# A fused Fourier-mixing and product-key-expert kernel: another order for the seven-product groups, routing in seven steps, and other slots for the preparation work

## The chip, the cores and the metric

The kernel runs on one core of one Trainium2 chip, as one launch. The metric is device time in microseconds (us), the median of several runs. TensorE is called PE here, VectorE DVE, ScalarE ACT, GpSimd POOL, and SyncE, which only issues transfers, SP.

## The reference

The input is x with 2048 rows and 512 columns. It is normalised to xn (mean and variance of each row), and three terms are added:

```python
return x + _A_ref(xn, A_dft_seq_re, A_dft_seq_im, A_dft_hid_re, A_dft_hid_im) + _B_ref(xn, B_w_q, B_k1, B_k2, B_u, B_v)
```

`_A_ref` is the real part of a two-dimensional discrete Fourier transform, given by its matrices. `_B_ref` is a layer of 4096 small experts. For each row and each of 32 heads it finds two experts and adds their outputs:

```python
q = jnp.einsum("nd,dhc->nhc", xf, w_q)            # H=32 heads, 2*128 columns
s1 = jnp.einsum("nhd,ed->nhe", q[..., :dk], k1)   # 64 scores
s2 = jnp.einsum("nhd,ed->nhe", q[..., dk:], k2)   # 64 scores
# the best 2 of s1 and of s2 give 4 candidates; the best 2 of their sums
# are the experts top_e = i1*64 + i2, with weights g = softmax(top_s)
act = _gelu(jnp.einsum("nd,nhkd->nhk", xf, u[top_e]))
out = jnp.einsum("nhk,nhk,nhkd->nd", g, act, v[top_e])
```

## The kernel before

The kernel is written with a tile framework: the program issues operations in order, and a scheduler places each engine's instructions by that order as their inputs come ready in its own estimate. On the chip each engine then works through its queue in order, so an instruction that waits holds all that stand behind it on its engine.

The time has four stages.

*Start* (up to some 80 us): normalisation, the Fourier transform by its symmetries, and the first scores.

*Scores* (some 80 to 427 us). The heads are handled in eight chunks of four heads (`NCH`), the rows in 16 tiles of 128 (`NT`). For each chunk j and tile i, `s_mm` (L252) issues 12 matmuls of 128x512 into a PSUM bank (`pa`, four buffers). In `scores` ACT copies the bank to a tile `ss` (L953, four buffers), and DVE takes from it the eight best values of each group of 64 (L957) and their indices (L961). Around that the loop over i issues other work at fixed tiles:

- `m_prep` (L162 and L164 on ACT, L167 on POOL) splits the projection weights of a later chunk into a high and a low half; `m_stage` and `m_mul` (L148, PE) need all four of them (t = 0 to 3) at tiles 3, 4, 5 and 7 of the chunk.
- `routing` turns the values and indices of the chunk that was just finished into two expert numbers and two weights. It came in three parts, issued behind tile 1 (part 0), tile 2 (part 2) and tile 4 (part 1) of the following chunk. In it POOL adds candidates (L886 to L888), DVE compares them (L889, L890), POOL subtracts (L891), ACT takes an Exp (L894), and DVE and POOL form the rest.
- `fill_uv` scales and splits u and v into halves (L780 and L781 on ACT, L782 on POOL) at the numbers in the list `slots`; for u four more POOL operations form sums (L810 to L813), and `split4` five tiles later splits these and stores them to DRAM (`s_d`). `stage_v` does the same for the v groups that stay in DRAM (`v_d`). `todo[n]` lists what is issued behind tile i of chunk j, with n = 16 j + i.

*Pairs* (some 427 to 1100 us). For 16 batches of 128 rows the kernel computes all products of the batch with u (4096 x 128), the phase "z", and the product of a sparse weighting with v, the phase "v". The phases run z0, z1, v0, then for b = 2, 4, ... 14: z(b, b+1), v(b-1), v(b), and at the end v15. A z phase of a pair takes two batches at once. Both factors are split in 2 x 2 blocks, and seven block products take the place of eight (Strassen's scheme in Winograd's form). The groups of u form four quads (`QUADS`), so there are 28 products of 24 matmuls each, issued by `slot` (L1172). A digit names the product and a letter the quad in the order `SEQ`. Products accumulate in three sums of a quad, each in a PSUM bank: X (products 1, 6, 7, 4), Y (2) and Z (5, 3). There are four such banks for all quads and for the sum of a v phase; `take` takes the one that was freed first. What drains them is listed in `work`: ACT copies behind 1 (L1206), 5 (L1211), 6 (L1213) and 7 (L1219), DVE adds behind 2 (L1208), 3 (L1216) and 7 (L1220, which adds what ACT's copy left), and ACT's gelu (L1196) behind 4. Products 3, 6 and 7 use sums of u from `s_d`, loaded into a ring of three tiles by `ring_load`, whose order `ring_plan` works out ahead. Products 1 and 5 and others use sums of x (`x4`, from `t_d`) or x itself (`xb2`), loaded at the start of the phase v(b-2).

A v phase has eight steps of 12 matmuls (L1334, `v_part`). Between the products and these steps the dictionary `plan` puts `g_mm` (DVE builds one-hot factors L, R in L1264, L1269, L1272; PE multiplies them, L1274), `w_part` (DVE L1282 and L1290, ACT L1289) and checks on the transform matrices and weights (`compare`, `fit`), which load tiles `cx` and `fit`. In a phase v(b-2) with even b-2, `w_part` for the batch b-1 is planned behind steps 5 and 7 and `g_mm` behind steps 1, 3 and 7. The last product of a pair, 4d, is issued behind step 0 of v(b-1).

*End* (from some 1100 us): the last v phase and the output.

These lines of the loop over tiles set the order of routing:

```python
if i in (1, 2, 4) and pend is not None:
    routing((0, 2, None, 1)[i - 1], *pend)
if j + 1 == NCH and i in (4, 7, 8):
    routing((4, 7, 8).index(i), j, vals, idx, 0, 4, nc.vector)
```

Of the kernel before, what the change touches and what calls it, by code (L numbers as in the profile page):

```python
# [18 lines left out]
P = 128  # L19
# [5 lines left out]
NCH = 8  # L25
# [11 lines left out]
def tile_fnet_peer(ctx, tc, x, ca, cb, c5, wt, wf, wr, wq, kt, ut, vn, out):  # L37
# [683 lines left out]
    def part_b(safe, stS, stP, stQ, stE, xt, u_sb, cmp_p, w4):  # L721
# [149 lines left out]
        def routing(part, j, vals, idx, t0=0, t1=NT, ge=nc.gpsimd):  # L871
# [11 lines left out]
            if part == 0:  # L883
# [4 lines left out]
                ge.tensor_tensor(c10, a[..., 1], b[..., 0], op=ALU.add)  # L888
                nc.vector.tensor_tensor(pm, c01, c10, op=ALU.is_ge)  # L889
                nc.vector.tensor_tensor(c01, c01, c10, op=ALU.max)  # L890
                ge.tensor_tensor(c00, c01, c00, op=ALU.subtract)  # L891
            elif part == 1:
                ex, g = c10, sp.tile([P, n, 2, HC], F32, tag="g", name=f"g{j}_{t0}", bufs=1)
# [3 lines left out]
                ge.tensor_tensor(g[:, :, 1, :], ex, g[:, :, 0, :], op=ALU.mult)  # L897
                nc.vector.tensor_copy(zi[:, :, 2, :, 0, hs], g)
                nc.vector.tensor_tensor(zi[:, :, 2, :, 1, hs], g, zi[:, :, 2, :, 0, hs], op=ALU.subtract)
            else:  # L900
                iw = sp.tile([P, n, 2, 2 * HC], F32, tag="if", name=f"if{j}_{t0}", bufs=1)
                i1 = iw.rearrange("p i w (k h) -> p i k w h", k=2)
                nc.vector.tensor_copy(iw, idx[:, :, :, 0:2].rearrange("p i w k h -> p i w (k h)"))
                if not safe:
                    v = iw.rearrange("p i w (k h) -> p (i w k) h", k=2)
                    ge.tensor_tensor(v, v, hoff.unsqueeze(1).to_broadcast([P, 4 * n, HC]), op=ALU.subtract)
                    c = j + (t0 > 0)
                    nc.vector.tensor_reduce(bnd[:, 0, c:c + 1], iw, axis=AX.XYZ, op=ALU.min)
                    nc.vector.tensor_reduce(bnd[:, 1, c:c + 1], iw, axis=AX.XYZ, op=ALU.max)
                di = sp.tile([P, n, 2 * HC], F32, tag="di", name=f"di{j}_{t0}", bufs=1)  # L910
# [6 lines left out]
                e = di.rearrange("p i (k h) -> p i k h", k=2).bitcast(I32)  # L917
# [85 lines left out]
        for g, n in zip(range(V2, 16), (25, 38, 41, 57, 73, 89, 102)):  # L1003
# [6 lines left out]
        for j in range(NCH):  # L1010
# [11 lines left out]
            for i in range(NT):  # L1022
# [15 lines left out]
                if i in (1, 2, 4) and pend is not None:  # L1038
                    routing((0, 2, None, 1)[i - 1], *pend)
                if j + 1 == NCH and i in (4, 7, 8):  # L1040
                    routing((4, 7, 8).index(i), j, vals, idx, 0, 4, nc.vector)
# [8 lines left out]
        for part in range(3):  # L1050
# [128 lines left out]
        def z_pair(b, n, after):  # L1179
# [3 lines left out]
            total, done, cg = 1344 * (len(SEQ) - 1), 0, 0  # L1183
            def work(at, o):
                if 1:
# [32 lines left out]
                    elif op == "7":  # L1218
                        nc.scalar.activation(dst(1, 1), v(X), AF.Copy)  # L1219
                        nc.vector.tensor_tensor(dst(1, 1), dst(1, 1), dst(1, 0), op=ALU.add)  # L1220
# [5 lines left out]

            for at, o in enumerate(SEQ[:-1]):
                while late and late[0][0] <= at:
                    late.pop(0)[1]()
                work(at, o)  # L1230
                done += 1344
                while cg < 16 and done * 16 >= (cg + 1) * total:
                    after(cg)
                    cg += 1

            def last():
                while late:
                    late.pop(0)[1]()
                work(len(SEQ) - 1, SEQ[-1])
                while late:  # L1240
                    late.pop(0)[1]()

            plan.setdefault((("v", b[0] - 1), 0), []).insert(0, last)
# [320 lines left out]
        if not safe:  # L1564
            for n in range(len(QUADS)):
                put(("v", 0), n, lambda qd=len(QUADS) - 1 - n: first_sum(qd))
# [32 lines left out]
        if not safe:  # L1599
# [18 lines left out]
            for f, n in ((U, 68), (F[0], NK + 16 - V2), (F[1], 16 + V2)):  # L1618
                assert sum(v.count(f) for v in plan.values()) >= n
        for n, ph in enumerate(phases):  # L1620
            if ph[0] == "z":
                b = ph[1:]
                for c in b:
                    ACT[c] = BT[c] if c < 2 else act_tile(c)
# [4 lines left out]
                if not safe and b[0] in PAIRS and len(b) == 2:  # L1629
                    z_pair(b, PAIRS.index(b[0]), after)  # L1630
# [178 lines left out]
```

## Time and profile before

| | before |
|---|---|
| median of 3 runs | 1151.65 us (1150.69 to 1154.37) |
| profiled execution, its own time | 1148.38 us |
| its span, first to last instruction | 1146.6 us |
| mean granted clock of PE | 0.993 |
| PE busy | 1111.1 us, 97% |
| DVE busy | 970.1 us, 85% |
| ACT busy | 681.0 us, 59% |
| POOL busy | 332.9 us, 29% |
| DMA, mean rate | 192 GB/s |

The table is read from the page of one profiled execution. PE's busy time is the sum over stages in which the same engine does different things, so what a change in one stage can bring is read from the idle time of PE in that stage. In a row of the timeline the first number is the start in us from the start of the span, the second the length in us, and what stands in square brackets is how long the engine stood idle just before and whose work ended that. The granted clock is the share of full speed at which PE was let run. The longer entries in the view of waits give total us, the number of times and the longest.

### The profile page before, as it was taken

What the parts mean: (1) busy time and instruction counts of PE and PEld (TensorE: products, weight loads), DVE (VectorE), ACT (ScalarE), POOL (GpSimd) and SP (SyncE); (2) the same over time, 40 slices, a digit from 0 to 9 for tenths busy, and PEclk for the clock granted to TensorE, in tenths of its full rate; (3) what the DMA queues carried; (4) which work ended last, traced back from release to release, by engine and by line L of the source; (5) the groups of instructions that cost most, each with busy time, mean ns of one, the idle gap of its engine ahead of it and who ended that gap; (6) DMA issues with size and microseconds to landing.
All of it is one profiled execution on the core that took longest, in us unless ns stands there. A gap on an engine that the chain in (4) does not pass through costs nothing.

```text
span 1146.6 us, 29162 instructions
## 1 busy us (share of the span) xinstructions
PE 1111.1 (97%) x11528; PEld 724.2 (63%) x11528; DVE 970.1 (85%) x2904; ACT 681.0 (59%) x1126; POOL 332.9 (29%) x385
## 2 busy tenths in 40 slices
PE   9999899999999999999999999999999999999997
PEld 6455454544445459779478579569559659659643
DVE  7899789899898799884997897898798788788783
ACT  6558498887888565455546546545545546555451
POOL 0429899988899740000000000000000000000000
PEclk8999999999999999999999999999999999999999
DMA  9883546454372325874866766757667667566354
GB/s 297 265 217 147 193 143 208 141 168 148 93 230 84 115 78 180 192 252 147 250 201 220 243 210 229 229 191 252 197 212 252 193 219 252 193 220 206 128 177 121
DMA packets 132273, 220.51 MB, mean 192 GB/s; under 512 B 35092, under 2 KB 71067, under 8 KB 132126
## 3 DMA queue, kind: packets, MB, share of 16 engines
q1 hardware_dynamic: 129520, 214.28, 58.0%
q0 software_dynamic: 2304, 4.20, 2.3%
q8 instruction: 92, 1.51, 0.5%
q14 instruction: 55, 0.45, 0.1%
q10 hardware_dynamic: 302, 0.08, 0.0%
HBM read 183.06 MB, written 29.69 MB: 186 GB/s over the span
## 4 chain that ended last, share of the span: by engine, by line
PE 42%; DVE 17%; DMA 8%; ACT 3%; issue 2%; POOL 2%; SPq 1%; DVEq 0%; ACTq 0%; POOLq 0%
PE z L1172 16%; PE v L1334 10%; PE s L252 9%; DMA cx<-in_cb_dram 4%; PE z L1095 4%; DVE L L1264 4%; DVE w L1282 3%; PE g L1274 2%; DVE act L1290 2%; DMA cx<-in_ca_dram 2%; DVE cx L1382 2%; DMA v<-v_d 1%; DVE w L1290 1%; DVE R L1269 1%; DVE R L1272 1%
## 5 line engine op out<-in xcount | busy, mean ns | idle before, releaser
L252 PE MATMUL s<-m,xq 128*128 128x512 f16 x1344 | 300.1, 382 | 5.4 <-ACT uvpFalse L122 3.1
L1334 PE MATMUL v<-v,act 128*128 128x512 f16 x1044 | 231.8, 379 | 1.4 <-DMA v<-v_d 1.4
L252 PEld LDWEIGHTS <-xq 128*128 128x128 f16 x1344 | 130.5, 99 | 158.3 <-issue 9.9
L1345 POOL DMA_DIRECT2D y<-in_x_dram x16 | 14.4, 898 | 660.9 <-DVE R L1269 144.2
L1334 PEld LDWEIGHTS <-act 128*128 128x128 f16 x1044 | 99.8, 98 | 116.7 <-issue 2.0
L1264 DVE TENSOR_TENSOR L<-io_lam,cmp 128x2048 f16<-128x2048 f16 x128 | 156.3, 1221 | 9.6 <-PE g L1274 9.6
L1172 PEld LDWEIGHTS <-u 128*128 128x128 f16 x2688 | 153.0, 98 | 4.9 <-issue 3.0
L957 DVE MAX8 vals<-ss 128x8 f32<-128x64 f32 x896 | 133.4, 216 | 3.6 <-ACT ss L953 3.5
L1172 PEld LDWEIGHTS <-s 128*128 128x128 f16 x1944 | 110.4, 98 | 8.4 <-issue 8.4
L1334 PE MATMUL v<-v,w 128*128 128x512 f16 x480 | 106.8, 379 | 1.4 <-DMA v<-v_d 1.4
L1408 ACT ACTIVATE cx<-cx 128x896 f32<-128x896 f32 x64 | 60.3, 942 | 62.7 <-DVE cx L1388 45.9
L953 ACT ACTIVATE ss<-s,wsc 128x512 f32<-128x512 f32 x120 | 79.8, 679 | 27.5 <-PE s L252 18.5
L961 DVE FIND_INDEX8 idx<-vals,ss 128x8 uint16<-128x256 f32 x224 | 93.8, 419 | 0.0
L1289 ACT ACTIVATE act<-w 128x1024 f16<-128x1024 f32 x36 | 48.4, 1359 | 63.4 <-DVE w L1282 59.6
L1172 PE MATMUL z<-xb,u 128*128 128x128 f16 x1344 | 84.2, 219 | 0.0
L1172 PE MATMUL z<-x,u 128*128 128x128 f16 x1344 | 81.4, 219 | 2.5 <-ACT act L1219 2.5
L1172 PE MATMUL z<-x,s 128*128 128x128 f16 x1296 | 81.1, 219 | 0.4 <-ACT act L1206 0.4
L1334 PEld LDWEIGHTS <-w 128*128 128x128 f16 x480 | 45.9, 98 | 54.6 <-issue 1.9
L1274 PEld LDWEIGHTS <-L 128*128 128x128 f16 x2048 | 60.7, 96 | 15.7 <-issue 3.7
L1282 DVE SCALAR_TENSOR_TENSOR w<-act,scl,g 128x1024 f32<-128x1024 f32 x44 | 55.9, 1280 | 16.0 <-ACT act L1196 16.0
L1274 PE MATMUL g<-R,L 128*128 128x32 f16 x2048 | 63.4, 176 | 3.9 <-DVE R L1272 3.0
L1196 ACT ACTIVATE act<-act,scl 128x512 f32<-128x512 f32 x56 | 39.8, 719 | 39.8 <-DVE act L1216 17.4
(365 smaller groups left out, 1910.2 us busy)
## 6 DMA issues: line engine op xcount, KB each, us to landing
v<-v_d SPq DMA_DIRECT2D x67, 512.0 KB, 5.1
s<-s_d SPq DMA_DIRECT2D x63, 512.0 KB, 4.4
cx<-in_cb_dram SPq DMA_DIRECT2D x64, 448.0 KB, 6.7
w<-in_wq_dram SPq DMA_DIRECT2D x28, 512.0 KB, 5.1
fit<-in_wq_dram SPq DMA_DIRECT2D x28, 512.0 KB, 3.8
uv<-in_vn_dram SPq DMA_DIRECT2D x16, 512.0 KB, 3.7
uv<-in_ut_dram SPq DMA_DIRECT2D x16, 512.0 KB, 4.1
s_d<-v SPq DMA_DIRECT2D x32, 256.0 KB, 4.2
```

The costliest lines, as they stand in the source:

```text
L252: nc.tensor.matmul(ps, xt[i][:, l, kd, :], m[:, r, kd, :], start=(n == 0), stop=(n == 3 * KD - 1))
L953: nc.scalar.activation(s, ps, AF.Copy, scale=inv)
L957: nc.vector.max(vals[:, i, w, :, h], s[:, g, :])
L961: nc.vector.max_index(idx[:, i, w].rearrange("p k h -> p (k h)"), vals[:, i, w, 0:2].rearrange("p k h -> p (k h)"), s[:, w * HC:g + 1, :]. ...
L1095: nc.tensor.matmul(ps if n == 1 else ps.rearrange("p (b n) -> p b n", b=2), ug[:, l, c % 2, kd, :], xb2[:, k0, r, kd, :] if n == 1 else xb ...
L1172: nc.tensor.matmul(bank[:, t * P:(t + 1) * P], lt, rt, start=(t == k == 0 and op in "125"), stop=(t == 3 and k == 5), skip_group_check=op ...
L1264: nc.vector.tensor_tensor(L.rearrange("p t (l two) -> p t l two", two=2), io_lam.rearrange("p (l two) -> p l two", two=2).unsqueeze(1).to_ ...
L1274: nc.tensor.matmul(p[:, hf, t * NC:(t + 1) * NC], L[:, t, :], R[:, t, :], start=True, stop=True)
L1282: nc.vector.scalar_tensor_tensor(w, act[:, :, ts], fw, p.rearrange("p h (n c) -> p c (h n)", c=NC), op0=ALU.mult, op1=ALU.mult)
L1289: nc.scalar.activation(w16[..., 0], w, AF.Copy)
L1334: nc.tensor.matmul(pv, w16[:, c, :, l], v_sb[g][:, r, cc, :], start=(n + cc == 0 and k == 0), stop=(n == end and cc == 1 and k == 2))
L1408: later.append(lambda: nc.scalar.activation(tf[:, P:], tf[:, P:], AF.Abs, accum_out=chk[:, n:n + 1]))
```

## The change

Four things change; the number of matmuls, of loads and of stores stays.

- `routing` has seven parts instead of three. For chunks before the last they are issued behind tiles 1, 2 (two parts), 4, 6, 8 and 10 of the following chunk: part 0 the adds, part 1 comparison, maximum and subtraction, parts 2 to 4 the indices, part 5 the Exp and the weights, part 6 their split. For the last chunk the parts are issued where the three parts were.
- The slots of `fill_uv`, of the sums behind it and of `stage_v` are others, and `m_prep` for chunks from 3 on is at tiles -4, -2, -1 and 1 relative to the start of the chunk ahead, instead of -4, -2, 0 and 2.
- The order `SEQ` of the 28 products is another, and so is the quad that each letter names (`turn_q`). The first three products of a pair, 1a, 5a and 2a, are issued behind steps 5, 6 and 7 of v(b-2), ahead of the other work planned there (`BEFORE` = 3); the last one stays behind step 0 of v(b-1) (`BEHIND` = 1). The work planned inside z is spread over the 24 products left there.
- Behind product 7 one DVE add reads the PSUM bank itself; ACT's copy is gone.

```diff
-                if i in (1, 2, 4) and pend is not None:
-                    routing((0, 2, None, 1)[i - 1], *pend)
+                if pend is not None:
+                    for r in ({1: (0, 1), 2: (2, 3, 4), 4: (5, 6)} if j + 1 == NCH else
+                              {1: (0,), 2: (1, 2), 4: (3,), 6: (4,), 8: (5,), 10: (6,)}).get(i, ()):
+                        routing(r, *pend)
...
-                    todo[(j - 1) * NT + 2 * t - (12 if j == 2 else 4)].append(
+                    todo[(j - 1) * NT + (2 * t - 12 if j == 2 else (-4, -2, -1, 1)[t])].append(
...
-        slots = [31, 33, 36, 45, 42, 48, 53, 57, 62, 67, 72, 77, 81, 86, 90, 95, 99, 104, 108, 112, 119, 121, 123, 124, 126]
+        slots = [31, 33, 36, 46, 43, 51, 55, 58, 67, 71, 74, 83, 87, 90, 99, 103, 106, 110, 113, 116,
+                 120, 122, 124, 125, 126]
...
-        for g, n in zip(range(V2, 16), (25, 38, 41, 57, 73, 89, 102)):
+        for g, n in zip(range(V2, 16), (25, 38, 41, 53, 69, 85, 101)):
...
-            SEQ = ("1a 5a 2a 6a 3a 1b 7a 2b 5b 4a 6b 3b 1c 7b 2c 5c 4b 6c 3c 1d 7c 2d 6d 5d 4c 7d 3d 4d").split()
+            SEQ = ("1a 5a 2a 6a 1b 3a 2b 7a 5b 6b 1c 4a 3b 7b 2c 5c 6c 1d 4b 3c 7c 5d 2d 6d 4c 3d 7d 4d").split()
+            BEFORE, BEHIND = 3, 1
...
-                return ("abcd" if n % 2 else "dcba").index(k)
+                return ((0, 3, 2, 1), (1, 3, 2, 0))[n % 2]["abcd".index(k)]
...
                     elif op == "7":
-                        nc.scalar.activation(dst(1, 1), v(X), AF.Copy)
-                        nc.vector.tensor_tensor(dst(1, 1), dst(1, 1), dst(1, 0), op=ALU.add)
+                        nc.vector.tensor_tensor(dst(1, 1), v(X), dst(1, 0), op=ALU.add)
                         gelu_late(dst(0, 1), 3)
...
+        def z_before(b, n, k):
+            if k == 0:
+                ACT[b] = act_tile(b)
+            ZP[b][0](k)
+
+        if not safe:
+            for n, b in enumerate(PAIRS):
+                ZP[b] = z_pair((b, b + 1), n)
+                for k in range(BEFORE):
+                    plan.setdefault((("v", b - 2), 8 - BEFORE + k), []).insert(0, lambda b=b, n=n, k=k: z_before(b, n, k))
+                for k in range(BEHIND):
+                    plan.setdefault((("v", b - 1), k), []).insert(0, lambda b=b, k=k: ZP[b][2](k))
```

More of the change, by code (lines that the diff above doesn't have):

```diff
@@ L891, in routing @@
                 ge.tensor_tensor(c00, c01, c00, op=ALU.subtract)
-            elif part == 1:
-                ex, g = c10, sp.tile([P, n, 2, HC], F32, tag="g", name=f"g{j}_{t0}", bufs=1)
+            elif part == 5:
+                RT["gg"] = sp.tile([P, n, 2, HC], F32, tag="g", name=f"g{j}_{t0}", bufs=1)
+                ex, g = c10, RT["gg"]
                 nc.scalar.activation(ex, c00, AF.Exp)
@@ L1049, in part_b @@
             pend = (j, vals, idx)
-        for part in range(3):
+        for part in (0, 1, 5, 6, 2, 3, 4):
             routing(part, *pend, 4, NT, nc.vector)
@@ L1177, in slot, with z_pair, work @@
                 used[0] += 1
-        def z_pair(b, n, after):
+        def z_pair(b, n):
             st = {}
             late = []
-            total, done, cg = 1344 * (len(SEQ) - 1), 0, 0
-            def work(at, o):
-                if 1:
+            total = len(SEQ) - BEFORE - BEHIND
+            def work(at):
+                if at < len(SEQ):
+                    o = SEQ[at]
+                    while late and late[0][0] <= at:
+                        late.pop(0)[1]()
                     op, qd = o[0], turn_q(o[1], n)
@@ L1225, in work, with middle, behind @@
                         banks.append(Xt)
-            for at, o in enumerate(SEQ[:-1]):
-                while late and late[0][0] <= at:
-                    late.pop(0)[1]()
[L1230 to L1243, printed above, removed]
+            def middle(after):
+                cg = 0
+                for k in range(total):
+                    work(BEFORE + k)
+                    while cg < 16 and (k + 1) * 16 >= (cg + 1) * total:
+                        after(cg)
+                        cg += 1
+            def behind(k):
+                work(BEFORE + total + k)
+                while k + 1 == BEHIND and late:
+                    late.pop(0)[1]()
+            return work, middle, behind
         GP = {}
@@ L1623, in part_b @@
                 for c in b:
-                    ACT[c] = BT[c] if c < 2 else act_tile(c)
+                    if c not in ACT:
+                        ACT[c] = BT[c] if c < 2 else act_tile(c)
                 def after(cg):
```

26 lines of the change are left out of this document (18 added, 8 removed).

## The prediction

> **What bounds the kernel now.** First the head of the page, for the engine with the least slack.
>
> ```profile
> span 1146.6 us, 29162 instructions
> ## 1 busy us (share of the span) xinstructions
> PE 1111.1 (97%) x11528; PEld 724.2 (63%) x11528; DVE 970.1 (85%) x2904; ACT 681.0 (59%) x1126; POOL 332.9 (29%) x385
> ```
>
> TensorE (PE) is busy in 1111.1 of 1146.6 us, and the change takes no matmul away. So it can win only from the 35.5 us in which PE waits, and from time in which PE runs at a lower clock. The view of waits, for PE alone, says who ended that idle time:
>
> ```profile
> PE z L1172 <- ACT act L1211: 5.2, 4, 1.7
> ...
> PE g L1274 <- DVE R L1272: 3.0, 4, 1.1
> PE v L1334 <- DMA v<-v_d: 2.8, 3, 1.4
> PE z L1172 <- ACT act L1219: 2.5, 4, 1.4
> PE z L1172 <- ACT w L1211: 2.3, 3, 1.7
> ...
> PE m L148 <- POOL w L167: 2.1, 2, 1.8
> ```
>
> The columns are total us, times, longest. In the stage of pairs PE waits 5.2 + 2.5 + 2.3 = 10.0 us before products (L1172), 2.8 before v tiles and up to 3.0 before g. In the score stage it waits 2.1 us for GpSimd's L167 and in the two places that the timeline of PE shows; its third row is an undisturbed tile:
>
> ```profile
> 122.81 4.18 PE L252 MATMUL s<-m,xq 128*128 128x512 f16 x12 [3.13 <-ACT uvpFalse L122]
> 264.02 4.37 PE L252 MATMUL s<-m,xq 128*128 128x512 f16 x12 [2.23 <-ACT ss L953]
> 352.83 2.75 PE L252 MATMUL s<-m,xq 128*128 128x512 f16 x12
> ```
>
> Twelve matmuls take 4.18 and 4.37 us behind the two stalls of 3.13 and 2.23 us, against 2.75. The view by windows says why (window, length, five engines, granted clock, DMA):
>
> ```profile
> 122.00:128.00 6.00, 5.19 (x38) 2.60 (x38) 3.12 (x16) 5.77 (x11) 4.70 (x13) 0.72 0.18 65
> 264.00:269.00 5.00, 4.98 (x37) 2.33 (x37) 5.00 (x22) 4.97 (x9) 3.71 (x7) 0.67 0.00 0
> ```
>
> The granted clock fell to 0.72 and 0.67, so the stalls cost a further 4.18 - 2.75 = 1.43 and 4.37 - 2.75 = 1.62 us. The Trainium skill (TensorE: Matmul & The Clock Gate, "What's actually happening") states that the clock halves after an idle window of about 3.4 us; by that neither stall would be charged and the gain below would be 3.0 us smaller. The trace disagrees: 2.23 us of idling sufficed.
>
> What held ACT before those stalls stands in its timeline; the third row is DVE's:
>
> ```profile
> 121.92 0.26 ACT L894 ACTIVATE c<-c 128x64 f32<-128x64 f32 x1 [6.64 <-POOL c L891]
> 262.10 0.26 ACT L894 ACTIVATE c<-c 128x64 f32<-128x64 f32 x1 [5.46 <-POOL c L891]
> 256.10 3.67 DVE L903 CAST if<-idx 128x256 f32<-128x256 uint16 x1
> ```
>
> Both times ACT stands 5 to 7 us at the Exp of routing (L894), which waits for GpSimd's subtraction L891, and that for DVE's comparison and maximum L889, L890. Behind the Exp in ACT's queue are the copies out of the score banks (L953) and that of the scale (L122), and PE waits for those banks.
>
> **The change, part by part.** *Routing in seven steps.* For chunks before the last, routing's first part was at tile 1 and its Exp at tile 4; now the adds are at tile 1, comparison and subtraction at 2, the Exp at 8, its last consumers at 10. No instruction is added. The Exp stands six tiles behind the subtraction in place of three; three tiles more are 3 x 2.75, 8 us, against a wait of 6.64 at most. What sits behind the Exp in ACT's queue is then not held. Gain: 3.13 + 2.23 + 1.43 + 1.62 = 8.4 us; low end 4 (one of the two stalls comes back in another place), high end 8.4.
>
> *Slots of sums and fills.* L167 is the end of `m_prep`, whose matmuls follow at tiles 3 to 7. The fourth prep of chunk 6 had slot 82, behind a fill at 81; it gets 81, ahead of the fill at 83, and all later chunks get the same pattern (fills at tiles 3, 7 and 10). Counts of ACT, GpSimd and DMA instructions stay. GpSimd is passed by one fill, its longest item (L782 and four sums behind it), which covers the longest of these waits, 1.8 us; who waits for the fill is only the next stage. Gain 2.1, low end 0. For the score stage that makes 10.5; I take 9.5, since GpSimd stays nearly full and a small wait may stay.
>
> *Seventh product from PSUM.* Per quad ACT's copy L1219 goes, and the DVE add reads PSUM instead.
>
> ```profile
> L1219 ACT ACTIVATE act<-z x20: 577/597/599, 512.9 to 1069.0; 128x512 f32<-128x512 f32 x20
> L1220 DVE TENSOR_TENSOR act<-act,w x12: 683/693/694, 513.5 to 1069.6; 128x512 f32<-128x512 f32 x12
> L1208 DVE TENSOR_TENSOR act<-z,act x16: 674/684/701, 594.7 to 974.2; 128x512 f32<-128x512 f32 x16
> DVE act L1220 <- ACT act L1219: 28.3, 16, 2.5
> ```
>
> L1208 is the same form with PSUM as a source: 684 ns against 693, so the add costs nothing more. ACT loses 28 x 0.6 = 17 us of work, and DVE 28.3 us of waiting for it. Neither is PE's time; both let banks drain earlier. Product 4 now waits for a DVE add where it waited for ACT's copy.
>
> *Another order, three products ahead.* A product is 24 matmuls, 1.34 us from start to start. Products that wait for a drain get more time: 5 to 3 has three products between in place of two, 6 to 7 three (quad d: two), 7 to 4 three or four (quads a, b). But the quads overlap more in the same four banks, and a bank is taken again sooner. Walking both orders: 1b takes the bank of 2a one product (and one g) after it, where another bank had been free for 6.7 us before; 5b, 2c, 5c, 1d, 5d and 2d take a bank two products (2.69 us) after its last, where it was three or four. How late the drains of one pair are now (PE, then DVE, then ACT; x48 is two products):
>
> ```profile
> 856.75 1.50 PE L1172 MATMUL z<-xb,u 128*128 128x128 f16 x24
> 865.59 2.84 PE L1172 MATMUL z<-x,u 128*128 128x128 f16 x48
> 870.90 1.50 PE L1172 MATMUL z<-xb,s 128*128 128x128 f16 x24 [1.13 <-ACT act L1211]
> 876.26 2.84 PE L1172 MATMUL z<-x,u 128*128 128x128 f16 x48
> 860.96 0.70 DVE L1208 TENSOR_TENSOR act<-z,act 128x512 f32<-128x512 f32 x1
> 871.37 0.68 ACT L1196 ACTIVATE act<-z,scl 128x512 f32<-128x512 f32 x1
> 882.00 0.67 ACT L1196 ACTIVATE act<-z,scl 128x512 f32<-128x512 f32 x1
> ```
>
> 2a begins at 856.75, so PE goes on at 858.09; its bank is drained at 861.66, 3.57 us later. In the new order 1.34 and a g of some 0.8 lie between: 1b would wait 1.4. 4a is issued by 868.27 and drained at 872.05, 3.78 later; 2c would wait 3.78 - 2.69 = 1.1. 4b: 878.94 to 882.67, 3.73; 5d would wait 1.0. 3b's wait of 1.13 goes. With drains as late as today a pair would wait 3.5 us in place of 1.1; six pairs make 21 against 10.0, a loss of 11. With drains half as late none of these waits is left, a gain of 10. I take a gain of 4, nearer the good end, as three rows make drains earlier: ACT loses 17 us, DVE 28.3 us of waiting, and the add of 2a, 3.6 us late since DVE lags in the v tiles ahead, gets three products (4.0 us) of PE time in those tiles. Not half as late, since ACT's queue also stands behind loads.
>
> *The v tiles.* The three products come after tiles 5, 6 and 7 of v(b-2), at the place where PE waits for a v load or for DVE's R:
>
> ```profile
> 850.40 2.75 PE L1334 MATMUL v<-v,w 128*128 128x512 f16 x12 [1.10 <-DMA v<-v_d]
> 1029.18 0.55 PE L1274 MATMUL g<-R,L 128*128 128x32 f16 x16 [1.07 <-DVE R L1272]
> s<-s_d SPq DMA_DIRECT2D x63, 512.0 KB, 4.4
> ```
>
> Two products ahead of tile 7 are 2.7 us, more than any one of these waits: gain 2.8 + 1.1 = 3.9, low end 0 if the loads start later too. I take 2.5. The moved products use no ring tile, so they issue no DMA and pass nothing on SP's queue. The x tiles they read are loaded at the start of v(b-2), five tiles (13 us) ahead of the first, and 512 KB land in 4.4.
>
> Sum: 9.5 + 4 + 2.5 = 16. The profiled execution took 1148.4 us, 1.8 more than its span, so 1132.4. It lies 3.3 under the median of the runs (1151.65), for which this makes 1135.7, said as 1136.
>
> **The rivals.** *The banks take it back.* Drains stay as late as today: 11 lost in the pairs, 9.5 won in the scores, 2.5 before v: 1151, no change. For it speaks that 1b has one product of slack; against it the DVE waits that go.
>
> *The add of 2a blocks DVE, slower.* It stands first among what is planned behind tile 7, ahead of w and g of batch b-1. If DVE's queue keeps that order, w, L and R cannot be built before PE has done 2a, and PE needs them right behind it. Price per pair: the add, 0.68, w (L1282) and its remainder, 1.31 each, and one L (L1264), with nothing to cover them:
>
> ```profile
> 845.99 1.31 DVE L1282 SCALAR_TENSOR_TENSOR w<-act,scl,g 128x1024 f32<-128x1024 f32 x1
> 847.91 1.26 DVE L1264 TENSOR_TENSOR L<-io_lam,cmp 128x2048 f16<-128x2048 f16 x1
> ```
>
> That is 0.68 + 2 x 1.31 + 1.26 = 4.6 us, in six pairs 27, on top of the 1135.7: 1163. It decides from 16/6 = 2.7 us per pair on. Against it: these two rows are 1.9 us apart though neither waits, so other work is interleaved, and the order on DVE is not simply that of the plan.
>
> *Routing spread out makes DVE late.* The CAST at 256.10 took 3.67 us, beside GpSimd's work; the rows of its line and of the stage (DVE is the third engine):
>
> ```profile
> L903 DVE CAST if<-idx x8: 186/286/3900, 161.5 to 434.7; 128x256 f32<-128x256 uint16 x6, 128x64 f32<-128x64 uint16 x1, 128x192 f32<-128x192 uint16 x1
> 103.24:386.00 282.76, 275.22 (x1780) 136.96 (x1778) 253.82 (x1299) 225.22 (x378) 253.04 (x283) 0.99 0.47 151
> ```
>
> Six places instead of three meet GpSimd's long operations more often: one more such delay of 3.6 us in each of six chunks would be 22 us of DVE, where 282.8 - 253.8 = 29 are free. It would be absorbed in part, and I take half the stage's 9.5 as lost: 1141. The Trainium skill (GPSIMD Engine Reference, "Key points") states that GpSimd contends with VectorE for SBUF when VectorE runs a two-port mode. The trace agrees, 0.29 us median against 3.9.
>
> **How the numbers follow.** My forecast (1136, own range 1129 to 1143) gets 0.60, the banks 0.15, DVE late by routing 0.12, DVE blocked by 2a 0.08, and 0.05 that every wait named goes: 10.5 + 10.0 + 3.9 = 24.4, so 1127. A difference of 0.3% (3.5 us) is about what a measurement here tells from none. Faster: 0.60 + 0.12 + 0.05 and 0.05 of the banks' case, 0.82. Same: the other 0.10 of the banks. Slower: 0.08. The range runs from 1127 to 1149, which leaves out the slower rival and half of the banks'.
>
> **What would show it.** Right: L894 no longer waits microseconds for L891, no wait of PE in the scores is over 1 us, and the granted clock stays 1.00 there; L1219 is gone and L1220 waits for PE; PE's waits before products name DVE adds or a gelu, some 6 us in all. Wrong: 1b late in every pair (banks), g late behind 2a (DVE's queue), or new waits of PE for `ss` (routing).

## The result, and the profile after

The changed kernel takes 1132.18 us (median of 4 runs, 1130.28 to 1135.99), against 1151.17 for the kernel before on the same chip (4 runs, 1149.61 to 1154.37). The ratio is 0.9836 [0.9802, 0.987] (in brackets, here and below, the 95% interval), 19 us faster where 16 were forecast. A second series of the same kernel gave 1132.76 and 0.9844 [0.9813, 0.9874].

The profiled execution of after took 1135.99 us, its slowest run, and that of before 1148.38, 2.8 below the median. Profile against profile shows only 12.4 of the 19 us. The head of the page and PE's waits in after:

```profile
span 1134.2 us, 29144 instructions
...
PE 1107.5 (98%) x11528; PEld 724.4 (64%) x11528; DVE 964.2 (85%) x2904; ACT 667.6 (59%) x1098; POOL 332.4 (29%) x385
```

```profile
PE z L1186 <- ACT act L1215: 4.3, 4, 1.3
PE z L1186 <- DVE act L1235: 2.6, 2, 2.2
PE g L1289 <- DVE R L1287: 2.5, 4, 1.0
PE z L1186 <- DVE w L1227: 2.3, 2, 1.6
PE z L1186 <- ACT w L1215: 1.9, 1, 1.9
PE s L252 <- ACT ss L962: 1.4, 2, 0.9
PE z L1186 <- DVE w L1235: 1.2, 1, 1.2
```

Lines are those of after: products L1172 are now L1186, g L1289, the gelu L1215, the add of product 2 L1227, of 3 L1235, of 7 L1238, the score copy L962, POOL's subtraction L892, the Exp L896. PE's wait for v loads (2.8) is gone. The waits for L167 and L122 are gone too, so the score stage has almost none left. But before products PE waits as long as ever: 4.3 + 2.6 + 2.3 + 1.9 + 1.2 = 12.3 us, where before had 10.8 (the prediction's 10.0 and two rows of 0.4).

By windows (the same stretches as before, then the two stages; window, length, five engines, granted clock, DMA), first after, then the two stages of before:

```profile
122.00:128.00 6.00, 6.00 (x51) 3.04 (x49) 3.05 (x16) 3.24 (x7) 5.17 (x16) 1.00 0.17 65
264.00:269.00 5.00, 5.00 (x46) 2.66 (x44) 4.93 (x32) 3.35 (x5) 4.46 (x6) 1.00 0.30 67
103.30:418.20 314.90, 313.01 (x1973) 154.45 (x1971) 284.04 (x1503) 250.30 (x415) 273.07 (x308) 1.00 0.46 147
465.50:1128.00 662.50, 646.75 (x8129) 463.42 (x8124) 546.73 (x972) 327.64 (x519) 14.20 (x17) 1.00 0.65 211
```

```profile
103.20:427.40 324.20, 316.66 (x1972) 155.77 (x1972) 289.81 (x1505) 252.45 (x419) 275.52 (x309) 0.99 0.45 143
476.20:1140.00 663.80, 646.30 (x8130) 461.98 (x8126) 546.72 (x971) 341.63 (x547) 14.20 (x17) 1.00 0.65 210
```

From the start of chunk 1 to the first product the score stage takes 314.9 us in place of 324.2: 9.3 less. The pairs, from the first step of v0 to PE's last matmul, take 662.4 in place of 664.0 (the windows are cut within 0.2 us of that). That profile of after is a long one: seven profiled kernels that have the new pairs unchanged run from 658.3 to 662.4 (median 659.8), so some 4 less than the one profile of before. Between the two stages, z0 and z1 went from 48.8 to 47.3.

### The profile page after: what moved, and what is told of

Its sections match the earlier page's. It is cut to its first block, busy times and chain, and to the rows that moved or that the text cites. A ratio compares the mean times of both kernels' runs of the same rounds, so it can differ in the third digit from the quotient of the medians.

```text
span 1134.2 us, 29144 instructions
## 1 busy us (share of the span) xinstructions
PE 1107.5 (98%) x11528; PEld 724.4 (64%) x11528; DVE 964.2 (85%) x2904; ACT 667.6 (59%) x1098; POOL 332.4 (29%) x385
## 4 chain that ended last, share of the span: by engine, by line
PE 64%; DVE 16%; DMA 8%; POOL 6%; ACT 3%; issue 2%; SPq 0%; ACTq 0%; POOLq 0%; DVEq 0%
PE s L252 19%; PE z L1186 18%; PE v L1349 18%; PE z L1108 4%; DMA cx<-in_cb_dram 3%; DVE L L1279 3%; PE g L1289 3%; DVE w L1297 2%; DMA fit<-in_wq_dram 2%; DVE act L1305 2%; PE m L148 1%; DVE w L1305 1%; POOL v L795 1%; DVE vals L966 1%; DVE R L1287 1%
## 5 line engine op out<-in xcount | busy, mean ns | idle before, releaser
L1186 PEld LDWEIGHTS <-u 128*128 128x128 f16 x2688 | 156.7, 98 | 20.2 <-issue 13.6
L1186 PEld LDWEIGHTS <-s 128*128 128x128 f16 x1944 | 110.6, 98 | 0.0
L1423 ACT ACTIVATE cx<-cx 128x896 f32<-128x896 f32 x64 | 60.2, 941 | 64.7 <-DVE cx L1403 48.9
L1186 PE MATMUL z<-xb,u 128*128 128x128 f16 x1344 | 84.8, 220 | 9.8 <-ACT act L1215 4.3
L962 ACT ACTIVATE ss<-s,wsc 128x512 f32<-128x512 f32 x120 | 80.1, 680 | 22.3 <-PE s L252 12.7
L1186 PE MATMUL z<-x,u 128*128 128x128 f16 x1344 | 85.1, 220 | 2.6 <-DVE act L1235 2.6
L1186 PE MATMUL z<-x,s 128*128 128x128 f16 x1296 | 81.1, 219 | 0.0
L1215 ACT ACTIVATE act<-act,scl 128x512 f32<-128x512 f32 x56 | 39.7, 719 | 52.7 <-DVE act L1235 27.2
L1297 DVE SCALAR_TENSOR_TENSOR w<-act,scl,g 128x1024 f32<-128x1024 f32 x44 | 55.9, 1281 | 16.1 <-ACT act L1215 16.1
L1289 PEld LDWEIGHTS <-L 128*128 128x128 f16 x2048 | 60.3, 96 | 13.5 <-issue 2.9
L1397 DVE TENSOR_TENSOR cx<-cx 128x512 f32<-128x512 f32 (+2 forms) x84 | 48.7, 615 | 22.1 <-DMA cx<-in_cb_dram 22.1
```

The costliest lines, as they stand in the source:

```text
L962: nc.scalar.activation(s, ps, AF.Copy, scale=inv)
L1186: nc.tensor.matmul(bank[:, t * P:(t + 1) * P], lt, rt, start=(t == k == 0 and op in "125"), stop=(t == 3 and k == 5), skip_group_check=op ...
L1289: nc.tensor.matmul(p[:, hf, t * NC:(t + 1) * NC], L[:, t, :], R[:, t, :], start=True, stop=True)
L1297: nc.vector.scalar_tensor_tensor(w, act[:, :, ts], fw, p.rearrange("p h (n c) -> p c (h n)", c=NC), op0=ALU.mult, op1=ALU.mult)
L1397: nc.vector.tensor_tensor(v, v, tv[:, 0:1].to_broadcast([P, len(ix), 256]), op=o)
L1423: later.append(lambda: nc.scalar.activation(tf[:, P:], tf[:, P:], AF.Abs, accum_out=chk[:, n:n + 1]))
```

## The experiments

Three questions: which part carries the gain of the scores; which part that of the pairs; and why PE still waits before products. Each kernel is after with one edit, unless said otherwise. They ran in three series, with their own runs of before: 1151.05 us (14 runs) for the first four kernels, 1149.65 (11) for the next four, 1150.96 (22) for the last four.

| kernel | median us | ratio to before [95%] | score stage us | pairs us |
|---|---|---|---|---|
| after_again | 1132.76 | 0.9844 [0.9813, 0.9874] | 315.0 | 659.0 |
| u_routing: old three parts of routing | 1134.39 | 0.9857 [0.9829, 0.9886] | 317.5 | 658.3 |
| u_slots: old slots and m_prep | 1143.85 | 0.9937 [0.9916, 0.9959] | 326.2 | 659.8 |
| u_order: old order, none ahead | 1137.13 | 0.9879 [0.9849, 0.9909] | 315.0 | 662.2 |
| u_before0: new order, none ahead | 1133.67 | 0.9856 [0.9834, 0.9878] | 314.9 | 659.7 |
| old_seq_before3: old order, three ahead | 1130.38 | 0.9837 [0.9817, 0.9858] | 314.9 | 657.6 |
| u_seventh: ACT's copy back | 1131.2 | 0.9847 [0.9825, 0.987] | 315.0 | 657.7 |
| fit3: a load of the v phases moved | 1136.5 | 0.9875 [0.9853, 0.9898] | 315.1 | 662.5 |
| fit_in_v: the pair's own load moved | 1137.42 | 0.9883 [0.9851, 0.9916] | 314.9 | 663.0 |
| u_mprep: old m_prep alone | 1138.32 | 0.99 [0.9867, 0.9932] | 319.5 | 661.2 |
| u_fills: old fills and stage_v alone | 1148.02 | 0.9993 [0.9974, 1.0013] | 329.2 | 659.6 |
| pairs_only: old routing, slots, m_prep | 1142.15 | 0.9933 [0.9912, 0.9954] | 325.7 | 662.2 |

### The scores: routing or slots

**after_again** is the changed kernel itself, for the spread.

> The changed kernel once more, unedited, as the yardstick of this group. Expected ratio to before 0.983 (0.980 to 0.987). In its profile the score stage (first product of z0) should again begin at about 418 us, against 427.4 before. If the pairs gain what the median says, and not the 1.6 us of the first profile, its pairs (first v step to the last matmul of PE) take 655 to 658 us, against 664.0 before; if the 662.4 us of the first profile are typical, the median's extra gain has another cause.

It repeated the result. Its pairs took 659.0 us, a little above the 655 to 658 that were expected if the median was typical.

**u_routing** puts routing's parts back to three places:

```diff
-                              {1: (0,), 2: (1, 2), 4: (3,), 6: (4,), 8: (5,), 10: (6,)}).get(i, ()):
+                              {1: (0, 1), 2: (2, 3, 4), 4: (5, 6)}).get(i, ()):
```

> The changed kernel with the old three places of routing (tiles 1, 2, 4). Theory A, the prediction's: routing carries 8.4 us, so this takes 8 us more than the changed kernel (1140), z0 begins near 426 us, and PE again shows two waits of 2 to 3 us behind an Exp, with the granted clock near 0.7 there. Theory B, from the first profile, in which the Exp stands at the same place of ACT's queue as before (11, 29, 42, 57, 73, 89 score copies ahead of it, before 10, 28, 43, 57, 73, 90): the places of routing matter little, the slots carry the gain, and this stays within 2 us of the changed kernel (1132 to 1134, z0 near 419).

The stage grew by 2.6 us and the time by 1.6, within the noise, as theory B had it. One stall is back, the one of chunk 1. Timeline of ACT in this kernel, then of PE:

```profile
121.11 0.26 ACT L896 ACTIVATE c<-c 128x64 f32<-128x64 f32 x1 [6.62 <-POOL c L892]
...
121.84 0.16 ACT L122 ACTIVATE uvpFalse<-uvs 128x2 f32<-128x2 f32 x1
```

```profile
122.00 2.75 PE L252 MATMUL s<-m,xq 128*128 128x512 f16 x12 [3.25 <-ACT uvpFalse L122]
```

ACT stands 6.62 us at the Exp with L122 behind it, as in before. The same place in after:

```profile
116.23 0.29 ACT L122 ACTIVATE uvpFalse<-uvs 128x2 f32<-128x2 f32 x1
116.53 1.28 ACT L896 ACT_TABLE_LOAD   x1
121.92 0.26 ACT L896 ACTIVATE c<-c 128x64 f32<-128x64 f32 x1 [4.11 <-POOL c L892]
```

The Exp starts at 121.92, to the hundredth as in before, and ACT still waits 4.11 us for POOL. What changed is that one score copy and L122 now stand ahead of it. Over the whole run ACT waits at the Exp as long as it did; first the rows of after, then of before:

```profile
ACT c L896 <- POOL c L892: 16.1, 5, 4.1
```

```profile
ACT c L894 <- POOL c L891: 16.1, 4, 6.6
```

The program issues the Exp four tiles later, yet counted in score copies ahead of it, it stands at place 11, 29, 42, 57 and 73 for the first five chunks, where before it was 10, 28, 43, 57 and 73. The framework's scheduler draws it forward. So the seven steps move the Exp by one tile at most.

**u_slots** takes the old slots and the old places of m_prep, with routing in seven steps:

```diff
-                    todo[(j - 1) * NT + (2 * t - 12 if j == 2 else (-4, -2, -1, 1)[t])].append(
+                    todo[(j - 1) * NT + 2 * t - (12 if j == 2 else 4)].append(
...
-        slots = [31, 33, 36, 46, 43, 51, 55, 58, 67, 71, 74, 83, 87, 90, 99, 103, 106, 110, 113, 116,
-                 120, 122, 124, 125, 126]
+        slots = [31, 33, 36, 45, 42, 48, 53, 57, 62, 67, 72, 77, 81, 86, 90, 95, 99, 104, 108, 112, 119, 121, 123, 124, 126]
...
-        for g, n in zip(range(V2, 16), (25, 38, 41, 53, 69, 85, 101)):
+        for g, n in zip(range(V2, 16), (25, 38, 41, 57, 73, 89, 102)):
```

> The changed kernel with the old slots of fills, sums, v staging and m_prep. Theory A: slots carry 2.1 us (the wait for L167), so 1134, z0 near 420, with the wait of PE for L167 of 1 to 2 us back. Theory B: the slots carry the gain of the score stage, because they set what stands ahead of routing in GpSimd's queue: 1139 to 1141, z0 near 426, with the wait at 264 us back.

The whole gain of the stage is gone: 326.2 us, 2.0 more than in before and 0.5 more than in pairs_only (below), which has the old routing too. The time is 11 us longer, more than either theory said. PE's waits in this kernel's timeline:

```profile
174.85 0.20 PE L148 MATMUL m<-sums,w 128*128 128x64 f16 x1 [3.00 <-POOL w L167]
...
265.29 2.75 PE L252 MATMUL s<-m,xq 128*128 128x512 f16 x12 [2.24 <-ACT ss L962]
...
321.73 0.20 PE L148 MATMUL m<-sums,w 128*128 128x64 f16 x1 [3.51 <-POOL w L167]
```

The stall of 2.23 us in chunk 4, which the prediction gave to routing, is there with seven steps (2.24). And PE waits 6.9 us for L167, where the two profiles with the old routing and the old slots show 2.1 (before) and 3.6 (pairs_only).

So the four corners, each from one profile, are: both old 324.2 (pairs_only 325.7), steps alone 326.2, slots alone 317.5, both 314.9. The slots carry the gain; the steps pay only with them, 2.6 us, at L122.

**u_mprep** and **u_fills** split u_slots: the first has only its edit of the m_prep line, the second only its edits of `slots` and of stage_v.

> The kernel after with the old places of m_prep alone (2t - 4 for t = 0 to 3 in place of -4, -2, -1, 1). With all slots old the score stage took 326.2 us and PE waited 6.9 us for L167 in three places. Theory A (the last prep stands behind a fill on GpSimd because of its own place): the waits for L167 come back, 5 to 7 us, and the time is 1138 to 1143. Theory B (the fills' slots alone decide): at most one wait for L167 of under 1 us, score stage 315 to 316.5, time 1131 to 1134.

> The kernel after with the old slots of fills and of stage_v, the new places of m_prep kept. Theory A (the place of m_prep decides): waits for L167 stay under 1 us in all, score stage 315 to 317, time 1131 to 1135. Theory B (the fills' slots decide): L167 is waited for 4 to 7 us, score stage 320 to 326, time 1137 to 1143. If both halves are needed, this run and the one with the old places of m_prep are each slower by 3 us or more.

Neither half does it alone. The third L167 of one chunk on POOL in after, then in u_mprep, and then u_mprep's PE around it:

```profile
164.48 2.14 POOL L167 TENSOR_TENSOR w<-w,wh 128x1024 f16<-128x1024 f32 x1
```

```profile
170.08 2.12 POOL L167 TENSOR_TENSOR w<-w,wh 128x1024 f16<-128x1024 f32 x1
```

```profile
156.72 5.34 PE L252 MATMUL s<-m,xq 128*128 128x512 f16 x24
...
172.26 0.20 PE L148 MATMUL m<-sums,w 128*128 128x64 f16 x1 [2.96 <-POOL w L167]
...
172.91 7.03 PE L252 MATMUL s<-m,xq 128*128 128x512 f16 x24
```

In after the third prep runs at 164.48, ahead of most of routing's index work on POOL (from L918 on). With the old place it is issued a tile later, falls behind them to 170.08, and PE waits 2.96 us for it. The 24 score matmuls behind that wait take 7.03 us in place of 5.34, so this one stall costs 4.6 us, all of the stage's growth (314.9 to 319.5). That is less waiting for L167 than theory A had (3.0 us in place of 5 to 7) at its price; theory B, that the fills alone decide, is out.

In u_fills the stage takes 329.2 us, more than with both halves old. PE waits 4.5 us for L167 and 7.7 for score copies, the longest at the end of the stage. ACT's timeline and PE's:

```profile
409.08 0.22 ACT L896 ACTIVATE c<-c 128x16 f32<-128x16 f32 x1 [7.85 <-DVE c L892]
```

```profile
410.96 20.63 PE L252 MATMUL s<-m,xq 128*128 128x512 f16 x84 [4.23 <-ACT ss L962]
```

ACT stands 7.85 us at the Exp of the last chunk's first routing, which waits for DVE, with score copies behind it. That wait is not new: it is 6.93 us in after, where PE loses 0.43 us behind it. In u_fills DVE had itself stood 2.64 us shortly before, for POOL's L899, which came behind the operations of a fill (0.99 us in after). The time, 1148.0 us, is above both forecasts. The places of m_prep and of the fills were wanted together; each old half was slower than after by 5 us or more (1138.32 and 1148.02).

### The pairs: which part

**pairs_only** has the old routing, slots and m_prep (the edits of u_routing and u_slots together).

> The kernel before with only the pairs changed (order, three products ahead, seventh product from PSUM); routing and slots are the old ones. Theory A (the parts add up): the score stage is that of before, 323 to 325 us, and the pairs give what is left of the whole change, 19 less 9.3 less 1.5, so about 8 us: 1142 to 1145. Theory B (the pairs by their profiles, 664.0 to 657.6 to 662.4, 2 to 6 us): 1145 to 1149. Theory C (the pairs give nothing, all is won in the scores): 1149 to 1152.

The ratio is 0.9933 [0.9912, 0.9954]: the pairs alone win 7.7 us [5.3, 10.1] of 1150.96. With its score stage at 325.7, as in before, the parts add up (theory A). The profiles show less for the pairs, some 4 us, theory B's share; this kernel's own profile is its slowest run (1147.61).

**u_order** undoes order and place, and keeps the add from PSUM:

```diff
-            SEQ = ("1a 5a 2a 6a 1b 3a 2b 7a 5b 6b 1c 4a 3b 7b 2c 5c 6c 1d 4b 3c 7c 5d 2d 6d 4c 3d 7d 4d").split()
-            BEFORE, BEHIND = 3, 1
+            SEQ = ("1a 5a 2a 6a 3a 1b 7a 2b 5b 4a 6b 3b 1c 7b 2c 5c 4b 6c 3c 1d 7c 2d 6d 5d 4c 7d 3d 4d").split()
+            BEFORE, BEHIND = 0, 1
...
-                return ((0, 3, 2, 1), (1, 3, 2, 0))[n % 2]["abcd".index(k)]
+                return ("abcd" if n % 2 else "dcba").index(k)
```

> The changed kernel with the old order of products, the old quads and no product ahead in v (the seventh product still added from PSUM). The prediction gives order and place 4 + 2.5 us together with the seventh product: 1136 to 1139, with the v_d waits (2.8 us) and a 5 to 3 wait of over 1 us per pair back. Rival (banks take it back): within 2 us of the changed kernel, since the first profile shows 12.3 us of waits before products against 10.8 before.

It is 4.4 us slower than after_again, as the prediction's side had it, though the two intervals overlap. V loads are awaited again, for 1.9 us, and g for 4.7; 3b waits 0.76 to 2.01 us for the copy of 5b in five pairs.

**u_before0** keeps the new order and sets `BEFORE, BEHIND = 0, 1`; **old_seq_before3** has the old `SEQ` and `turn_q` with `BEFORE` = 3; **u_seventh** puts ACT's copy back (below, what was expected of each, in this order):

```diff
-                        nc.vector.tensor_tensor(dst(1, 1), v(X), dst(1, 0), op=ALU.add)
+                        nc.scalar.activation(dst(1, 1), v(X), AF.Copy)
+                        nc.vector.tensor_tensor(dst(1, 1), dst(1, 1), dst(1, 0), op=ALU.add)
```

> The changed kernel with its new order of products, but none ahead in the v tiles (all of them behind v(b-2), as before). Undoing order and place together cost 4.4 us (1137.1 against 1132.8). Theory: the place is worth the waits that stood behind tile 7, 2 to 3 us: 1135 to 1136, the v_d waits (1.9 us) and g waits (4.7 us) of that run come back, and DVE's add of 2a is again over 2 us late. Rival: the place is worth nothing by itself (what it saves before v is paid at 1b): 1132 to 1134.

> The changed kernel with the old order and the old quads, but the first three products ahead in the v tiles. Theory: the waits of 3b for the copy of 5b (about 1.2 us in each of five pairs) come back and the waits of 2c for the gelu of 4a go, so order alone is worth 0 to 2 us: 1133 to 1135. Rival: the order carries most of the 4.4 us, since the looser chains absorb ACT's delay: 1136 to 1137.

> The changed kernel with ACT's copy behind product 7 again and the add from the copy. ACT gets 17 us of work back and DVE waits for it. Theory: the drains get later, 4 waits for DVE and 2c for 4: 2 to 4 us more, 1135 to 1137. Rival: ACT's and DVE's slack in the pairs hides it, since what makes 4a late is a load and not the copy: within 1.5 us of the changed kernel.

None of the three differs from after (0.9836, 0.9844) beyond the intervals: 0.9856, 0.9837, 0.9847. The first and the third landed in the range of their rivals, the second below both of its ranges. So neither the order, nor the place, nor the add from PSUM shows a share of its own; a share of some 2 us would be hidden in these intervals. The waits show why. In u_before0, then in old_seq_before3, within the pairs:

```profile
PE g L1289 <- DVE R L1287: 6.3, 9, 1.2
```

```profile
PE z L1186 <- ACT act L1232: 4.3, 4, 1.8
PE z L1186 <- ACT act L1225: 3.2, 4, 1.3
PE z L1186 <- ACT w L1232: 1.5, 2, 1.0
```

Without products ahead, the waits before products fall to 3.6 us, but g is waited for 6.3. With the old order and three ahead, g falls to 1.4 and products wait 10.0, of which 9.0 for ACT's copies. PE's waits in the pairs come to 11 to 15 us in each of these kernels (16.6 in before); mostly their owner changes.

### Why PE still waits before products

In after, 2c waits 0.78 to 1.92 us for the gelu of 4a in pairs 1 to 5 (the seven pairs are counted from 0). Pair 4, on ACT and then on PE:

```profile
861.65 1.06 ACT L1475 ACTIVATE fit<-fit 128x1024 f32<-128x1024 f32 x1 [3.75 <-DMA fit<-in_wq_dram]
...
862.71 0.58 ACT L1225 ACTIVATE act<-z 128x512 f32<-128x512 f32 x1
863.19 0.68 ACT L1215 ACTIVATE act<-z,scl 128x512 f32<-128x512 f32 x1
```

```profile
863.92 1.50 PE L1186 MATMUL z<-xb,u 128*128 128x128 f16 x24 [1.29 <-ACT act L1215]
```

ACT waits 3.75 us for a load of the weight check `fit`, with the copy behind 1c and the gelu of 4a queued behind it. Two runs move such loads. **fit3** moves one of the even v phases from step 7 to step 3:

```diff
-                    for cg, f in enumerate((None, F[1], F[1], U, U, U, U, F[0]) if ph[1] % 2 == 0 else (
+                    for cg, f in enumerate((None, F[1], F[1], F[0], U, U, U, U) if ph[1] % 2 == 0 else (
```

> The changed kernel with one check step moved: in v phases of even batches the step that loads a tile of w_q to be checked (fit) is issued behind step 3 instead of step 7, and the steps of compare that stood at 3 to 6 behind 4 to 7. Nothing is left out. In the first profile ACT stood 3.75 us at the Abs of such a tile (860 us), with the copy of 1c and the gelu of 4a behind it, and 2c waited 1.29 us for that gelu; the same in five pairs (1.17, 0.78, 1.92, 1.29, 1.06). Theory (a late load on ACT's queue makes 2c wait): the waits of 2c go, 4 to 6 us less, 1127 to 1129. Rival (another load or the DVE work of compare takes its place): 1131 to 1135.

It was the wrong load, and with 1136.5 us the run is above both forecasts. The timeline of ACT in fit3 shows the same wait at the same place, and PE's shows what comes of it:

```profile
860.74 1.06 ACT L1475 ACTIVATE fit<-fit 128x1024 f32<-128x1024 f32 x1 [5.26 <-DMA fit<-in_wq_dram]
```

```profile
863.00 1.50 PE L1186 MATMUL z<-xb,u 128*128 128x128 f16 x24 [2.10 <-ACT act L1215]
```

In this profile two waits of 2c, of 2.39 and 2.10 us, were each followed by 3.41 us at half clock. The load that ACT waits for is planned inside the pair, at step 8 of 16. **fit_in_v** takes that one out of the pair:

```diff
-                    put(ph, 8, F[0])
...
-                            None, F[1], F[0], None, U, U, U, F[0])):
+                            None, F[1], F[0], F[0], U, U, U, F[0])):
```

> The kernel after, but the fit whose load is issued in the middle of each pair (step 8 of 16) stands at tile 3 of the odd v tile behind the pair. In the kernel after, ACT waits 3.75 us for that load at 861.65 with two drains of products behind it, and the earlier run with another fit moved left that wait as it was (5.26 at 860.74, up to 5.3 in each pair). Theory A (the place of this load in ACT's queue is what makes 2c late): ACT's long waits for the load go, PE's waits of 2c for the gelu L1215 (7.0 us, 4 times in that run, 1.17 to 1.92 a pair in the kernel after) go too, some 5 us of waits are gone, so 1127 to 1129 at the median and the stage of pairs under 656. Theory B (2c is late because its bank has only two products of time in the new order, with or without the load): the waits for L1215 stay within 1 us a pair and the time stays at 1131 to 1134.

ACT's long waits for `fit` are gone (2.55 at most), and theory A's time still failed: 1137.42 us, and products wait 12.7 us. Its mechanism held in part. In pairs 3 to 6 the gelu of 4a now ends 0.8 us behind its product, where after had 2.4 to 4.6, and 2c doesn't wait; but there 5c waits 0.45 to 1.99 us for DVE's add of 3. And in pair 2 another check stands ahead of the gelu. This kernel on ACT, then on PE:

```profile
686.02 0.95 ACT L1423 ACTIVATE cx<-cx 128x896 f32<-128x896 f32 x1 [5.99 <-DVE cx L1403]
...
686.97 0.67 ACT L1215 ACTIVATE act<-z,scl 128x512 f32<-128x512 f32 x1
```

```profile
687.69 2.72 PE L1186 MATMUL z<-xb,u 128*128 128x128 f16 x24 [4.17 <-ACT act L1215]
```

The next check in line, L1423 of `compare`, took the load's place: ACT stood 5.99 us at it, and PE waited 4.17 for the gelu behind it. Before that, DVE's part of the check had waited 0.90 and 2.08 us for loads of `cx`. From 686.38 on the clock was halved for 6.83 us; the 24 matmuls in the row took 2.72 us, where 1.50 is usual. Theory B as it was written (two products are too few, with or without a load) is out as well, since without the load 2c doesn't wait in pairs 3 to 5. What both runs and after share is a check, placed ahead of a drain by the scheduler and not ready. Kernels without any checks in the pairs were not run.

## Why the prediction was right, and where not

**Scores, 9.5 forecast, 9.3 measured.** The size held and its shares did not, so that the sum came out this close is luck. The step that failed is "The Exp stands six tiles behind the subtraction in place of three ... What sits behind the Exp in ACT's queue is then not held". It was read from the order in which the program issues, and the scheduler drew the Exp forward again: it waits 16.1 us for POOL, as before. Of the 8.4 us given to the seven steps the runs leave 2.6, at L122. The slots, given 2.1 for L167, carry 6.7 alone (324.2 to 317.5), and with them the stall of chunk 4 is gone. The Exp of that chunk in after, on ACT, where its wait was 5.46:

```profile
253.79 0.26 ACT L896 ACTIVATE c<-c 128x64 f32<-128x64 f32 x1 [2.63 <-POOL c L892]
```

The sign to look for, "L894 no longer waits microseconds for L891", failed, while "no wait of PE in the scores is over 1 us" and the clock of 1.00 came true (0.9 at most, 1.00 in both stretches). The right outcome came by another route.

**The clock's 3.0 us** (1.43 + 1.62 in the forecast) isn't a fixed price: a stall of 3.25 us in u_routing was followed by twelve matmuls in 2.75 us, full speed. The traces show what sets it. In each of the 14 the half-speed stretches start and end on one grid of 3.413 us and are one to three steps of it long (the last one is cut by the end of the trace). Views by windows, each window one step of that grid: around the stall of 2.23 us in before, and around that of 3.25 us in u_routing.

```profile
260.51:263.92 3.41, 1.28 (x27) 0.95 (x26) 3.41 (x19) 1.82 (x4) 2.46 (x7) 1.00 0.43 147
263.92:267.33 3.41, 3.31 (x8) 1.17 (x8) 3.41 (x12) 3.38 (x8) 2.50 (x4) 0.50 0.00 0
```

```profile
116.67:120.08 3.41, 2.07 (x31) 1.27 (x30) 3.21 (x14) 0.00 (x0) 3.41 (x6) 1.00 0.16 52
120.08:123.49 3.41, 1.50 (x7) 0.68 (x7) 1.24 (x5) 2.38 (x4) 3.17 (x7) 1.00 0.26 97
123.49:126.91 3.42, 3.42 (x38) 1.97 (x37) 2.72 (x14) 3.39 (x8) 2.47 (x8) 1.00 0.07 24
```

The granted clock is the third number from the end. In before PE was busy for 1.28 of the 3.41 us, so it stood idle for 2.13 in one step, and the next step ran at 0.50. In u_routing an edge of the grid parts the stall: PE idled 1.34 us in one step and 1.91 in the next, and the clock stayed at 1.00. The stall of 3.00 us in u_slots had 2.73 us in one step and was charged; its stall of 2.24 us was parted into 1.22 and 1.01 and was not. Over all 14 traces, from 60 us on and counting waits of over 0.15 us, each of the 12 full-speed steps with 2.03 us or more of idling was followed by a half-speed step. Of the 50 with 1.2 to 1.92 us two were: 1.92 in after, at 772.41, and 1.56 in u_before0, at 837.68. A half-speed step loses 3.41 / 2 = 1.7 us, so the two in before's score stage are 3.4 of the 9.3 us won there.

The prediction said that the trace disagrees with the Trainium skill (TensorE: Matmul & The Clock Gate, "What's actually happening"), by its window of 3.4 us. The same section says that the window is free-running, and the grid of the traces agrees. But a window need not be idle throughout here: 2.03 us in one were enough.

**Pairs, 4 + 2.5 forecast, 7.7 [5.3, 10.1] measured** in pairs_only. The sum is near; the steps are not all shown. The wait for v loads went as forecast, 2.8 to none, and g fell from 3.0 to 2.5 (1.6 in the second profile). "PE's waits before products name DVE adds or a gelu, some 6 us in all": the names are right, the size is not, 12.3 and 10.5 us in the two profiles. That the drains would come earlier is the step behind it, and it held for one product and not for the other. The add of 2a ends 0.8 us behind its product in six of the seven pairs, where before had 2.7 to 4.2. The gelu of 4a is as late as it was: 3.4 to 4.6 us in pairs 1 to 5, before 3.5 to 4.2. ACT did lose L1219 (28 instructions, 1126 to 1098), and DVE now waits 4.7 us in all for PE at the seventh product, where it waited 28.3 + 8.2 = 36.5 for ACT (the prediction counted the first of the two rows; the second is the last one here):

```profile
DVE act L1238 <- PE z L1186: 3.5, 6, 0.6
...
DVE w L1238 <- PE z L1186: 1.2, 2, 0.6
```

```profile
DVE w L1220 <- ACT w L1219: 8.2, 5, 1.8
```

That alone moved no time that these runs can tell: u_seventh has the copy back and takes 1131.2 us. Of the 12.3 us, 6.2 are waits for the gelu of 4a, which stands behind ACT's stops at the checks; the other 6.1 are waits for DVE's adds, and no run took those apart. The walk of pair 4 was right in one place (2c, 1.1 forecast, 1.29 measured), and wrong there for 1b (1.4, none) and 5d (1.0, none). In pair 0, where the add of 2a is still 2.9 us late, 1b did wait 1.64 us for it.

Why the pairs' profiles show some 4 us of the 7.7 isn't settled. Before has one profile, 2.8 us better than its median, which would make up most of the gap. This is an argument and was not measured. The 1.5 us between the stages (z0 and z1) was in no step. It goes with the slots of the fills: 48.0 us in pairs_only, 47.5 and 47.6 in u_fills and u_slots, 47.3 in all others.

**The rivals.** The prediction prices them for six pairs; the kernel has seven (28 copies L1219, four a pair), so the loss of 11 us would be 14.5 and the 27 us would be 32. Neither came. The banks took back no more than the waits that stayed. 2a does not block DVE. The end of 2a on PE, and DVE's timeline in after:

```profile
844.78 1.50 PE L1186 MATMUL z<-xb,u 128*128 128x128 f16 x24
```

```profile
846.39 0.69 DVE L1227 TENSOR_TENSOR act<-z,act 128x512 f32<-128x512 f32 x1
847.00 1.21 DVE L1279 TENSOR_TENSOR L<-io_lam,cmp 128x2048 f16<-128x2048 f16 x1
```

The add runs 0.11 us behind PE's end, and L follows without a gap. 1b starts at 848.26 and finds the bank drained. Routing did not make DVE late: DVE is busy 284.04 us in the stage in place of 289.81, and the longest CAST of that line takes 2.49 us in place of 3.90.

## What to carry to other kernels

Where a scheduler orders each queue, read an instruction's place from the trace of its engine (what stands ahead of it) and not from where the program issues it: an Exp issued four tiles later started at the same hundredth of a microsecond. A part that pays nothing alone can be needed by another, so undo parts singly and together before giving each its share. And when one blocker is taken out of a queue, look at what stands next: here another check took the place at once, and PE's longest wait for the gelu grew from 1.9 to 4.2 us.

## What was not expected of the hardware

The same kernel on the same chip is granted another mean clock from run to run: in the first series 0.991 to 0.998 over 14 runs of before (1145.85 to 1155.91 us) and 0.995 to 1.000 over 6 of after (1131.53 to 1136.76). Half-speed steps are a part of that. The engines' queues in after and in u_order hold the same instructions in the same order for the first 290 us. In after PE waited 1.02 us for a load at 9.29 us and the clock was halved for 6.83 us from 11.24 on. In u_order neither came, and chunk 1 began at 101.34 us in place of 103.25. So one profile can miss its median by several microseconds, as that of after does by 3.8. What a stall costs beyond its length depends on where it falls in the grid: parted by an edge, one of 3.25 us (u_routing) was free, and one of 1.92 us within a step (after, 772.41) was not.
